# First channel product of the last batch as seven products for eight, and a newly drawn task order

## The chip, the cores and the metric

The kernel runs on one core of one Trainium2 chip. The core has five engines with an instruction queue each: TensorE (PE, matmuls, whose weight loads are shown apart as PEld), VectorE (DVE), ScalarE (ACT), GpSimd (POOL) and SyncE (SP, which here only issues transfers). Each works through its own queue in order and waits on semaphores that the others raise. The metric is the device time of one execution in microseconds, taken as the median over runs; lower is better.

## The reference

Sliding-window attention with sink tokens, then one MLP block that mixes over tokens and over channels. Batch is 4, 8 heads, 768 tokens, head size 64 (so 512 channels), 2048 hidden channels. Cut to what matters:

```python
scores = q @ k.T / sqrt(64); keep = (pos < 4) | (0 <= i - j < 128)
x   = softmax(where(keep, scores, -1e9)) @ v          # heads side by side: (4, 768, 512)
a1  = alpha1 * x + beta1
u   = x + lam * einsum('ts,bsd->btd', w_tok, a1)      # token mixing
a2  = alpha2 * u + beta2
h   = maximum(a2 @ w_ch1, 0.0)                        # first channel product, 512 -> 2048
out = u + lam * (h @ w_ch2)                           # second channel product, 2048 -> 512
```

## The kernel before

All four batches go through the same stages, and the stages of neighbouring batches overlap. Names ending in a number of batch, such as `uT3` or `hT3`, are the tiles of that batch.

- **Attention** (`scores`, `pv`): per block of 128 keys, scores go to PSUM (L724), ACT takes the exponential into `E` (L746), DVE or POOL masks it (L761, L686), PE multiplies with `vfs` (L825) and DVE divides by the sum (L850, L851) into `x`. POOL and DVE make `xh`, the input of token mixing, out of `x` (L869, L872; L860 in batch 0). In batch 0 q and k are loaded at the start, half of them by POOL's casting transfers (L497), transposed on PE (L611, L614) and copied out to `qkT` by ACT or DVE (L356, L358).
- **Token mixing** (`tok`, L956): six row tiles per batch, six matmuls of 128x512 each; DVE adds the result to `x` (L963), ACT or POOL casts it to `u16` (L356, L358). `uT` is its transpose, by PE in batch 0 (`uTp`, L997) and by transfers in the later batches; ACT or DVE then applies alpha2 and beta2 (L980, L982). A batch's 768 tokens are kept as two chunks of 384.
- **First channel product** (`mlp1`, L1036): for each chunk and each of 16 tiles of 128 hidden channels, four matmuls of 128x384 accumulate in one PSUM buffer, and one eviction on ACT (L1042) or DVE (L1044) applies the relu into `hT`. So a batch has 32 tiles and 128 matmuls. The weights are `w1f`, loaded as half precision by POOL's queue (L555).
- **Second channel product**: batch 0 does it plainly (`mlp2`, L1221). Batches 1 to 3 (`STRASSEN`) use `prod` (L1153): the product of 2x2 blocks is formed out of seven block products P1 to P7 instead of eight, with sums of blocks of `hT` (`h_sums`, S1 to S4, L1094 to L1097, all on DVE) and sums of blocks of the weights (`w2_sums`, L1068, once). P1 is read out, P2 accumulates on top of P1, and so on; DVE adds the results to `x` (L1166, L1184, L1189, L1192) and SP stores it.

The order of instructions is not written by hand. Each stage adds tasks to a `Plan` with a priority `p`, the engines that may take it with a cost for each, what it comes after, and the buffers that it uses. `Plan.run` is a list scheduler: it steps through time by those costs, and at each step takes the task that can start earliest, ties by priority, on the engine that is done with it first, giving it a free buffer. What it returns is the order in which instructions are emitted, and so the order of each engine's queue. `since`, `SEEN` and the transfer model `Rings` are part of that costing. `homes` says how many buffers there are of a kind: four PSUM banks of kind `d`, two pairs of banks of kind `S`, four buffers `n16` and four `wst`, and so on. While PE would stand idle in the first 36 us, `idle` puts in small matmuls on a tile of zeros (L349). `PAR` shifts groups of priorities, and `TURNS` is a list of seeds: `shuffle` adds random amounts to a share of the priorities, once per seed.

In the last batch nothing else is left to interleave: the program order there is token mixing among the last products of batch 2, then the 32 tiles of the first product, then the seven products of the second and the stores.

Of the kernel before, what the change touches and what calls it, by code (L numbers as in the profile page):

```python
# [9 lines left out]
FP32 = mybir.dt.float32  # L10
# [101 lines left out]
class Plan:  # L112
# [18 lines left out]

    def run(self, prio):

# [34 lines left out]
        def pick():  # L168
            best = None
            spare = {k: sorted(h for h, x in zip(homes[k], busy[k]) if not x) for k in homes}  # L170
            for r, i in open_:
                at = ready[i]
                if best is not None and at > best[0]:
                    continue
                t = tasks[i]
                asked = {}
                for b in t.uses:
                    if b.home is None:
                        asked[b.kind] = asked.get(b.kind, 0) + 1
                if any(len(spare[k]) < n for k, n in asked.items()):  # L180
                    continue
                at = max([at] + [spare[k][n - 1] for k, n in asked.items()])
                own = None
                for e in t.engs:
                    at_e = max(free[e], at)
                    if e == POOL or (e == DVE and t.port):
                        at_e = max(at_e, port)
                    key = (at_e + FW * t.engs[e], at_e, r, at_e + t.engs[e], i, e)
                    if own is None or key < own:
                        own = key  # L190
                if best is None or own[1:] < best:
                    best = own[1:]
            return best
# [51 lines left out]

    def emit(self, turns):

        prio = [t.prio for t in self.tasks]
        for seed in turns:
            prio = shuffle(prio, seed)  # L250
        for t, e, start, stop, idle in self.run(prio):
            t.at = (e, start, stop)
# [3 lines left out]
            for b in t.uses:  # L256
                if b.t is None:
                    pool, shape, dtype = self.pools[b.kind]
                    b.t = pool.tile(b.shape or shape, b.dtype or dtype,
                                    tag=f"{b.kind}_{b.home}", bufs=1, name=b.name)  # L260
            t.fn(e)


# [16 lines left out]
def kernel(  # L280
# [135 lines left out]

    TURNS = (13523, 134113, 50022, 128275, 136711, 187603, 125671, 100730, 14946, 163131, 178432, 158827, 183776, 137680, 153375, 26742, 367527, 307353, 376563, 212018, 255075, 397706, 218147, 375675, 393913, 224567, 207692, 352780, 243076, 346008)
    W1_SINCE = 20000.0
# [609 lines left out]
    def mlp1(p, b, chk, fi):  # L1028
        if fi == 0:
            hT[b, chk] = Buf("hT", None, None, f"hT{b}_{chk}")  # L1030
# [21 lines left out]
    HD = DM // 2  # L1052
    lo_, hi_ = slice(0, HD), slice(HD, DM)

    w2s = {}
# [248 lines left out]
    STEP = 100.0  # L1304
    PAR = {'lead': 50.0, 'lo0': 20, 'hi0': 16, 'lo': -20, 'hi': 30, 'lead3': 42.0, 'w2s': 10, 'p7': 2, 'hs': 0, 's2': 2, 'w2p': 9}
    for b in range(B):
# [10 lines left out]
        else:  # L1317
            seq = [("tok", ti) for ti in range(NR)]
            m1 = [("m1", 0, fi) for fi in range(NF)]
            m1 += [("m1", 1, fi) for fi in range(NF)]  # L1320
        seq += m1
        if b in STRASSEN:
            def two(u, w):
                return [("pr", a, nt) for a, nt in ((u, 0), (u, 1), (w, 0), (u, 2), (w, 1), (w, 2))]

            seq += two("P1", "P2")
            i = seq.index(("m1", 1, 8))
            seq[i:i] = [("hs", "S3")]
            i = seq.index(("pr", "P1", 0))
# [19 lines left out]
        for i, (what, *args) in enumerate(seq):  # L1349
# [6 lines left out]
            if what == "pr" and args[0] in ("P7", "P4"):  # L1356
                p -= PAR["p7"]
            {"tok": tok, "uT": uTp, "m1": mlp1, "m2": mlp2, "hs": h_sums, "pr": prod}[what](p, b, *args)
            if b and what == "tok":
                uTx(p + 0.3, b, *args)  # L1360
        if b + 1 == STRASSEN[0]:
            w2_sums(w0 + ns + PAR["w2s"])
# [30 lines left out]

    plan.emit(TURNS)

# [34 lines left out]
```

The softmax here doesn't subtract the row's maximum and nothing guards it: scores larger than these inputs give would overflow.

## Time and profile before

The median of 14 runs is 256.65 us (256.48 to 258.74). The profiled execution took 256.95 us, of which the span on the core is 255.2.

| stretch (us of the span) | what PE does there | PE busy | DVE busy | ACT busy | POOL busy |
|---|---|---|---|---|---|
| 0 to 15.46 | loads arrive, transposes, fillers | 13.24 | 10.22 | 7.79 | 7.51 |
| 15.46 to 30.49 | attention of batch 0 | 15.03 | 12.38 | 14.48 | 11.57 |
| 30.49 to 60 | token mixing and first product of batch 0 | 28.40 | 24.90 | 21.20 | 8.36 |
| 60 to 104 | rest of batch 0, attention of batch 1 | 42.83 | 34.46 | 23.34 | 17.53 |
| 104 to 212.6 | batches 1 and 2, attention and token mixing of 3 | 108.15 | 86.73 | 59.75 | 42.35 |
| 212.6 to 252 | both channel products of the last batch | 39.28 | 20.06 | 16.06 | 0.61 |
| 252 to 255.2 | last add and stores | 0.00 | 0.34 | 0.00 | 0.00 |

A line of groups gives source line, engine, operation, output and input tiles, shapes, count, then busy time and mean nanoseconds of one, and the idle time of the engine before it. The busy time of a stretch merges rows that overlap: an instruction's row can begin before the row ahead of it has ended, so durations add up to more than the time they fill. The chain of waits is the chain of work that ended last, followed back from the last instruction. In a timeline line the first figure is the start in the span, the second the length.

### The profile page before, as it was taken

What the parts mean: (1) busy time and instruction counts of PE and PEld (TensorE: products, weight loads), DVE (VectorE), ACT (ScalarE), POOL (GpSimd) and SP (SyncE); (2) the same over time, 40 slices, a digit from 0 to 9 for tenths busy, and PEclk for the clock granted to TensorE, in tenths of its full rate; (3) what the DMA queues carried; (4) which work ended last, traced back from release to release, by engine and by line L of the source; (5) the groups of instructions that cost most, each with busy time, mean ns of one, the idle gap of its engine ahead of it and who ended that gap; (6) DMA issues with size and microseconds to landing.
All of it is one profiled execution on the core that took longest, in us unless ns stands there. A gap on an engine that the chain in (4) does not pass through costs nothing.

```text
span 255.2 us, 5519 instructions
## 1 busy us (share of the span) xinstructions
PE 246.9 (97%) x2174; PEld 160.6 (63%) x2174; DVE 189.1 (74%) x402; ACT 142.6 (56%) x236; POOL 87.9 (34%) x108
## 2 busy tenths in 40 slices
PE   8899998999999999899999999999999999999994
PEld 7654645675545544456678676558668766667883
DVE  6677997596878878578889997877789764136782
ACT  2689845989848035688971225867571125775000
POOL 7409802344445330169653450735310101000000
PEclk9999999999999999999999999999999999999999
DMA  6999999998943899699679689501000256000105
GB/s 200 198 211 323 214 248 389 374 356 187 224 79 114 178 247 209 119 207 228 145 140 179 127 184 256 89 3 21 3 0 3 60 166 146 0 0 3 63 4 185
DMA packets 86130, 38.80 MB, mean 152 GB/s; under 512 B 73540, under 2 KB 80460, under 8 KB 86104
## 3 DMA queue, kind: packets, MB, share of 16 engines
q1 hardware_dynamic: 82320, 35.14, 56.5%
q0 software_dynamic: 3744, 3.28, 8.0%
q8 instruction: 17, 0.28, 0.5%
q14 instruction: 9, 0.07, 0.1%
q10 hardware_dynamic: 40, 0.03, 0.1%
HBM read 29.91 MB, written 6.29 MB: 142 GB/s over the span
## 4 chain that ended last, share of the span: by engine, by line
PE 88%; DMA 4%; DVE 3%; POOL 1%; issue 1%; ACT 1%; POOLq 0%; ACTq 0%
PE h L1036 33%; PE P L1153 21%; PE tok L956 11%; PE ch L1221 8%; PE pv L825 5%; PE S L724 4%; DMA n<-in_q_dram 4%; PE S L719 1%; DVE uT L982 1%; PE tp L614 1%; PE pv L818 1%; POOL n L497 1%; PE wT L916 1%; ACT uT L980 1%; DVE w2f L1068 1%
## 5 line engine op out<-in xcount | busy, mean ns | idle before, releaser
L1036 PE MATMUL h<-uT,w1f 128*128 128x384 f16 x512 | 91.9, 326 | 2.7 <-DVE uT L982 1.3
L1036 PEld LDWEIGHTS <-w1f 128*128 128x128 f16 x512 | 47.3, 98 | 34.4 <-issue 5.5
L1042 ACT ACTIVATE hT<-h 128x384 f16<-128x384 f32 x99 | 48.4, 493 | 25.9 <-PE h L1036 25.5
L1153 PEld LDWEIGHTS <-hT 128*128 128x128 f16 x408 | 39.8, 98 | 6.7
L746 ACT ACTIVATE E<-S 128x1024 f16<-128x1024 f32 (+1 forms) x39 | 37.9, 1001 | 7.5 <-PE S L724 3.7
L869 POOL TENSOR_TENSOR tm<-x,la_b 128x512 f32<-128x512 f32 x18 | 26.2, 1454 | 26.3 <-DVE xh L872 19.2
L956 PE MATMUL tok<-xh,wtokT 128*128 128x512 f16 x144 | 33.4, 379 | 0.0
L356 ACT CAST u<-x 128x512 f16<-128x512 f32 x19 | 11.7, 618 | 30.2 <-DVE x L963 30.0
L1153 PE MATMUL P<-w2f,hT 128*128 128x256 f16 x216 | 25.9, 273 | 0.0
L1166 DVE TENSOR_TENSOR x<-x,P 128x256 f32<-128x256 f32 x45 | 18.3, 417 | 8.2 <-PE P L1153 8.0
L1044 DVE TENSOR_SCALAR hT<-h 128x384 f16<-128x384 f32 x29 | 15.8, 553 | 11.6 <-PE h L1036 11.2
L956 PEld LDWEIGHTS <-wtokT 128*128 128x128 f16 x144 | 13.9, 98 | 14.7
L1221 PE MATMUL ch<-w2f,hT 128*128 128x512 f16 x96 | 23.0, 379 | 0.0
L1153 PE MATMUL P<-w2s,hT 128*128 128x256 f16 x192 | 22.8, 273 | 0.0
L851 DVE TENSOR_TENSOR x<-pv,rec 128x256 f32<-128x256 f32 x48 | 20.4, 424 | 1.7
L358 POOL CAST vfs<-vnat 128x512 f16<-128x512 f32 x18 | 15.0, 842 | 16.5 <-DMA vnat<-in_v_dram 16.4
L963 DVE TENSOR_TENSOR x<-x,tok 128x512 f32<-128x512 f32 x24 | 16.2, 684 | 5.7 <-PE tok L956 5.7
L356 ACT CAST n<-nat 128x768 f16<-128x768 f32 x16 | 13.2, 829 | 11.9 <-DMA nat<-in_q_dram 8.9
L825 PEld LDWEIGHTS <-E 128*128 128x128 f16 x328 | 15.2, 97 | 6.0 <-issue 1.6
L825 PE MATMUL pv<-vfs,E 128*128 128x65 f16 x328 | 17.9, 194 | 0.0
L358 POOL CAST u<-x 128x512 f16<-128x512 f32 x5 | 3.1, 622 | 34.1 <-DVE x L963 21.1
L1221 PEld LDWEIGHTS <-hT 128*128 128x128 f16 x96 | 8.6, 98 | 9.0 <-issue 0.2
(131 smaller groups left out, 325.5 us busy)
## 6 DMA issues: line engine op xcount, KB each, us to landing
out_dram<-x SPq DMA_DIRECT2D x21, 256.0 KB, 2.9
nat<-in_q_dram SPq DMA_DIRECT2D x13, 384.0 KB, 5.6
nat<-in_k_dram SPq DMA_DIRECT2D x13, 384.0 KB, 5.6
vnat<-in_v_dram SPq DMA_DIRECT2D x18, 256.0 KB, 4.8
wst_w<-in_moe_w_ch_dram SPq DMA_DIRECT2D x8, 512.0 KB, 7.8
wtn<-in_moe_w_tok_dram SPq DMA_DIRECT2D x6, 384.0 KB, 4.2
w1f<-in_moe_w_ch_dram POOLq DMA_DIRECT2D x4, 512.0 KB, 10.1
v<-in_v_dram SPq DMA_DIRECT2D x12, 128.0 KB, 7.0
```

The costliest lines, as they stand in the source:

```text
L356: nc.scalar.copy(o, i)
L358: engine[e].tensor_copy(o, i)
L746: nc.scalar.activation(eT.t, pS.t[:, :, 0 : n * w].rearrange("p e (i w) -> p e i w", i=n), AF.Exp, scale=scale)
L825: nc.tensor.matmul(po.t[:, hl, :], eT.t[:, e_, off + i, c : c + P], vf[j][:, h, :], start=(r < 2 and n == 0), stop=(n == len(parts) - 1 an ...
L851: nc.vector.tensor_mul(bx.t[:, 4 * G : 4 * G + 4, :], po.t[:, :, 0:D], rec.t.to_broadcast([P, 4, D]))
L869: engine[e].tensor_mul(bt.t, bx.t.rearrange("p h d -> p (h d)"), la1_b)
L956: nc.tensor.matmul(pt.t, wtokT[:, si, ti * P : (ti + 1) * P], hs[si].t, start=(si == 0), stop=(si == NR - 1))
L1036: nc.tensor.matmul(ph.t, w1f[:, c, fi * P : (fi + 1) * P], bu.t[:, c, chk * NTOK : (chk + 1) * NTOK], start=(c == 0), stop=(c == NC - 1))
L1042: nc.scalar.activation(bh.t[:, fi, :], ph.t, AF.Relu)
L1153: nc.tensor.matmul(pc.t, hh[:, nt * P : (nt + 1) * P], w(fi), start=(first and n_ == 0), stop=(n_ == HF - 1), skip_group_check=True)
L1166: nc.vector.tensor_add(row(bx)[:, cols], row(bx)[:, cols], pc.t)
L1221: nc.tensor.matmul(pc.t, bh.t[:, fi, nt * P : (nt + 1) * P], w2f[:, fi, :], start=(fi == 0), stop=(fi == NF - 1))
```

## The change

In the last batch (`HSUM = 3`) the first channel product is done as seven products for eight too, for six of the eight pairs of hidden tiles. A pair is tile i and tile i + 8 for both chunks, so a 2x2 block product: two hidden tiles, two chunks, the 512 channels in two halves. The tiles 0, 1, 8 and 9 (`NPL = 2`) stay as they were, through `mlp1`.

- `w1_sums` makes S1 to S4 of blocks of `w1f`, eight instructions of 128x768. S1, S2 and S4 go to three buffers of kind `wst`; S3 is written into `w1f` in place, so it comes after the last tile of batch 2 that reads the same columns.
- `u_sums` makes T1 to T4 of blocks of `uT`, four instructions of 128x768, into the four `n16` buffers.
- `mlp1_pair` adds the seven products of a pair, each of two matmuls of 128x384. P1, P6, P5 and P3 accumulate one after another in one PSUM bank (V); P1, P6 and P5 are read out into buffers `ha`, `hb` and `hc` (kinds `vnat` and `x`) before the next may accumulate. P7 and P4 share the other bank of the pair (Q), P2 has a buffer of kind `d`. DVE adds `ha` to P2, `hc` to P7 and `hb` to P7 + P4 into `hT`, each followed by a relu in place on DVE, POOL or ACT; P3's bank is evicted with a relu as before.
- In the last batch S3 of the second product is placed before P1 instead of among the tiles.
- The order: `Plan.run` takes a list `pin` that can bind a task to one of its engines, a new function `nudge` changes priorities and pins from a seed, and the kernel lists 188 such seeds (`NUDGES`). `TURNS` differs from the seventeenth seed on, and `PAR` has other values. All tasks of the kernel are reordered by this, those of the start included: POOL's first casting load of q comes ahead of its work on `sel`, SP's first load is q instead of a tile of w_tok, ACT takes seven of the eight copies to `qkT` of batch 0 (five before) and three of six to `wtokT` (two before). Of the eight sums of `w1f`, six stand among the token adds of batch 1 and two among those of batch 3.

The engine totals of the program: 500 matmuls of 128x384 for the first product (512 before), 99 fillers (106), 429 instructions on DVE (399), 240 on ACT (242), 130 on POOL (113). The source lines move: L1036 becomes L1088, L1153 becomes L1326; the 84 matmuls of the pairs are L1181.

```diff
--- before.py
+++ after.py
@@ -129,7 +129,7 @@
-    def run(self, prio):
+    def run(self, prio, pin=None):
         tasks = self.tasks
         rank = [0] * len(tasks)
@@ -181,7 +181,10 @@
                     continue
                 at = max([at] + [spare[k][n - 1] for k, n in asked.items()])
                 own = None
-                for e in t.engs:
+                one = pin[i] if pin and pin[i] <= len(t.engs) else 0
+                for n, e in enumerate(t.engs):
+                    if one and n + 1 != one:
+                        continue
                     at_e = max(free[e], at)
                     if e == POOL or (e == DVE and t.port):
                         at_e = max(at_e, port)
@@ -243,12 +246,15 @@
         self.ends = free
         return steps
-    def emit(self, turns):
+    def emit(self, turns, nudges):
         prio = [t.prio for t in self.tasks]
         for seed in turns:
             prio = shuffle(prio, seed)
-        for t, e, start, stop, idle in self.run(prio):
+        pin = [0] * len(prio)
+        for seed in nudges:
+            nudge(prio, pin, seed)
+        for t, e, start, stop, idle in self.run(prio, pin):
             t.at = (e, start, stop)
...
+def nudge(prio, pin, seed):
...
+    kind = mix() % 6
+    w = wide[mix() % 8]
+    c = mix() % n
+    def by():
+        a = unit()
+        return (a + unit() - 1.0) * w
+    if kind == 0:
+        prio[c] += by()
+    elif kind == 1:
+        for _ in range(2 + mix() % 5):
+            i = (c + mix() % 60) % n
+            prio[i] += by()
...
+    elif kind == 4:
+        pin[c] = mix() % 3
+    else:
+        prio[c] += by()
+        i = (c + mix() % 30) % n
+        pin[i] = mix() % 3
 def shuffle(prio, seed):
@@ -414,7 +465,8 @@
     PAIRS = 3
-    TURNS = (13523, 134113, 50022,
...
-        26742, 367527, 307353, 376563,
...
-        243076, 346008)
+    TURNS = (13523, 134113, 50022,
...
+        26742, 354967, 310655, 266923,
...
+        392681, 339225)
+    NUDGES = (514892687, 622207306, 64711582,
...
+        192761335, 155598846)
     W1_SINCE = 20000.0
     V0 = (((0, 1), (2, 3), (4, 5)), ((0, 1, 2), (3, 4, 5)))
@@ -1026,7 +1078,7 @@
                 [done["uTd", b, 3 * chk + i] for i in range(3)] + [done["ab2"]], [bo])
     def mlp1(p, b, chk, fi):
-        if fi == 0:
+        if (b, chk) not in hT:
             hT[b, chk] = Buf("hT", None, None, f"hT{b}_{chk}")
         bh, bu = hT[b, chk], uT[b, 0]
         ph = Buf("d", [P, NTOK], FP32, f"h{b}_{chk}_{fi}")
@@ -1051,6 +1103,127 @@
     HF = NF // 2
     HD = DM // 2
     lo_, hi_ = slice(0, HD), slice(HD, DM)
+    HSUM = 3
+    NPL = 2
+    w1s = {}
+    uS = {}
+    pair = {}
+    def w1_sums(p):
+        n = (HF - NPL) * P
+        f, k_ = slice(NPL * P, HF * P), slice((HF + NPL) * P, NF * P)
+        for w in ("S1", "S2", "S4"):
+            w1s[w] = Buf("wst", [P, 2, n], FP16, f"w1{w}")
+        b1, b2, b4 = w1s["S1"], w1s["S2"], w1s["S4"]
+        late = [done["h", HSUM - 1, chk, fi] for chk in range(2) for fi in range(HF + NPL, NF)]
+        for c in range(2):
+            def sub(q, name, made, after, uses, c=c):
+                done["w1" + name, c] = add(
+                    p + 4 * c + q, {DVE: 600, POOL: 2000}, lambda e: made(engine[e], c), after, uses, port=True)
+            sub(0, "S1", lambda g, c: g.tensor_add(b1.t[:, c], w1f[:, c, k_], w1f[:, 2 + c, k_]), [done["w1", 3]], [b1])
+            sub(1, "S2", lambda g, c: g.tensor_sub(b2.t[:, c], b1.t[:, c], w1f[:, c, f]), [done["w1S1", c]], [b1, b2])
+            sub(2, "S4", lambda g, c: g.tensor_sub(b4.t[:, c], w1f[:, 2 + c, f], b2.t[:, c]), [done["w1S2", c]], [b2, b4])
+            sub(3, "S3", lambda g, c: g.tensor_sub(w1f[:, c, k_], w1f[:, c, f], w1f[:, c, k_]),
+                [done["w1S1", c]] + late, [])
+    def u_sums(p, b):
+        bu = uT[b, 0]
+        for w in ("T1", "T2", "T3", "T4"):
+            uS[w] = Buf("n16", [P, 2, NTOK], FP16, f"u{w}")
+        t1, t2, t3, t4 = (uS[w] for w in ("T1", "T2", "T3", "T4"))
+        c0, c1 = slice(0, NTOK), slice(NTOK, S)
+        ud = lambda chk, h: [done["uT", b, chk, 2 * h + c] for c in range(2)]
+        def sub(q, name, made, after, uses):
+            done["u" + name] = add(p + q, {DVE: 500, POOL: 1500}, lambda e: made(engine[e]), after, [bu] + uses, port=True)
+        sub(0, "T3", lambda g: g.tensor_sub(t3.t, bu.t[:, 2:4, c1], bu.t[:, 0:2, c1]), ud(0, 0) + ud(1, 0) + ud(1, 1), [t3])
+        sub(0.1, "T1", lambda g: g.tensor_sub(t1.t, bu.t[:, 0:2, c1], bu.t[:, 0:2, c0]), ud(0, 0) + ud(1, 0), [t1])
+        sub(0.2, "T2", lambda g: g.tensor_sub(t2.t, bu.t[:, 2:4, c1], t1.t), [done["uT1"]] + ud(1, 1), [t1, t2])
+        sub(0.3, "T4", lambda g: g.tensor_sub(t4.t, bu.t[:, 2:4, c0], t2.t), [done["uT2"]] + ud(0, 1), [t2, t4])
+    def mlp1_pair(p, b, what, i):
+        if what == "P1":
+            for chk in range(2):
+                if (b, chk) not in hT:
+                    hT[b, chk] = Buf("hT", None, None, f"hT{b}_{chk}")
+            pair[i] = [Buf("S", None, None, f"hp{i}"), Buf("d", [P, NTOK], FP32, f"h{b}_0_{i}")] + [
+                Buf(k_, [P, NTOK], FP32, f"h{w}{i}") for k_, w in (("vnat", "a"), ("vnat", "b"), ("x", "c"))]
+        two, px, ba, bb, bc = pair[i]
+        bu = uT[b, 0]
+        f, k_ = slice(i * P, (i + 1) * P), slice((HF + i) * P, (HF + i + 1) * P)
+        fs = slice((i - NPL) * P, (i - NPL + 1) * P)
+        c0, c1 = slice(0, NTOK), slice(NTOK, S)
+        lhs, rhs, after, into, uses = {
+            "P1": (lambda c: w1f[:, c, f], lambda c: bu.t[:, c, c0], [done["w1", i // 4]], "V", []),
+            "P2": (lambda c: w1f[:, 2 + c, f], lambda c: bu.t[:, 2 + c, c0], [done["w1", i // 4]], "X", []),
+            "P3": (lambda c: w1s["S4"].t[:, c, fs], lambda c: bu.t[:, 2 + c, c1], [done["w1S4", c] for c in range(2)], "V", [w1s["S4"]]),
+            "P4": (lambda c: w1f[:, 2 + c, k_], lambda c: uS["T4"].t[:, c], [done["uT4"]], "Q", [uS["T4"]]),
+            "P5": (lambda c: w1s["S1"].t[:, c, fs], lambda c: uS["T1"].t[:, c], [done["uT1"]] + [done["w1S1", c] for c in range(2)], "V", [w1s["S1"], uS["T1"]]),
+            "P6": (lambda c: w1s["S2"].t[:, c, fs], lambda c: uS["T2"].t[:, c], [done["uT2"]] + [done["w1S2", c] for c in range(2)], "V", [w1s["S2"], uS["T2"]]),
+            "P7": (lambda c: w1f[:, c, k_], lambda c: uS["T3"].t[:, c], [done["uT3"]] + [done["w1S3", c] for c in range(2)], "Q", [uS["T3"]]),
+        }[what]
+        if what in ("P1", "P2", "P3"):
+            after = after + [done["uT", b, what == "P3", c] for c in ((0, 1) if what == "P1" else (2, 3))]
+        first = what in ("P1", "P2", "P7")
+        po = px if into == "X" else two
+        def acc():
+            return px.t if into == "X" else two.t[:, "VQ".index(into), 0:NTOK]
+        def mm(e):
+            for c in range(2):
+                nc.tensor.matmul(acc(), lhs(c), rhs(c), start=first and c == 0, stop=c == 1, skip_group_check=True)
+        before = {"P6": "P1", "P5": "P6", "P3": "P5", "P4": "P7"}.get(what)
+        if before:
+            after = after + [done["hread", before, i]]
+        if what == "P7":
+            after = after + [done["hp", "P1", i]]
+        a = done["hp", what, i] = add(p, {PE: 2 * 163}, mm, after, [po, bu] + uses)
+        def read(bx):
+            return add(p + 0.05, {ACT: 493, DVE: 556}, lambda e: copy(e, bx.t, acc()), [a], [po, bx])
+        def plus(bx, chk, fi, more, acc=acc):
+            bh = hT[b, chk]
+            r = add(p + 0.05, {DVE: 556}, lambda e: nc.vector.tensor_add(bh.t[:, fi, :], bx.t, acc()), [a] + more, [po, bx, bh])
+            def relu(e):
+                if e == ACT:
+                    nc.scalar.activation(bh.t[:, fi, :], bh.t[:, fi, :], AF.Relu)
+                else:
+                    engine[e].tensor_scalar_max(bh.t[:, fi, :], bh.t[:, fi, :], 0.0)
+            done["h", b, chk, fi] = add(p + 0.06, {DVE: 300, POOL: 600, ACT: 493}, relu, [r], [bh], port=True)
+            return r
+        if what == "P1":
+            done["hread", "P1", i] = read(ba)
+        elif what == "P2":
+            plus(ba, 0, i, [done["hread", "P1", i]])
+        elif what == "P6":
+            done["hread", "P6", i] = read(bb)
+        elif what == "P5":
+            done["hread", "P5", i] = r = read(bc)
+            done["hread", "P7", i] = plus(bc, 1, HF + i, [r, done["hp", "P7", i]], lambda: two.t[:, 1, 0:NTOK])
+        elif what == "P4":
+            plus(bb, 0, HF + i, [done["hread", "P6", i]])
+        elif what == "P3":
+            bh = hT[b, 1]
+            def relu(e):
+                if e == ACT:
+                    nc.scalar.activation(bh.t[:, i, :], acc(), AF.Relu)
+                else:
+                    nc.vector.tensor_scalar_max(bh.t[:, i, :], acc(), 0.0)
+            done["h", b, 1, i] = add(p + 0.05, {ACT: 493, DVE: 556}, relu, [a], [po, bh])
     w2s = {}
@@ -1302,7 +1475,7 @@
     STEP = 100.0
-    PAR = {'lead': 50.0, 'lo0': 20, 'hi0': 16, 'lo': -20, 'hi': 30, 'lead3': 42.0, 'w2s': 10, 'p7': 2, 'hs': 0, 's2': 2, 'w2p': 9}
+    PAR = {'lead': 46.0, 'lo0': 20, 'hi0': 16, 'lo': -12, 'hi': 26, 'lead3': 58.0, 'w2s': -20, 'p7': 2, 'hs': 3, 's2': 0, 'w2p': 9, 'mp': 1.3, 'us': 15, 'w1s': -30}
     for b in range(B):
         w0 = STEP * b
         if b == 0:
@@ -1318,14 +1491,23 @@
             seq = [("tok", ti) for ti in range(NR)]
             m1 = [("m1", 0, fi) for fi in range(NF)]
             m1 += [("m1", 1, fi) for fi in range(NF)]
+            if b >= HSUM:
+                own = [fi for h in range(2) for fi in range(HF * h, HF * h + NPL)]
+                m1 = [("m1", chk, fi) for chk in range(2) for fi in own] + [("us",)]
+                order = ("P1", "P7", "P2", "P6", "P5", "P4", "P3")
+                m1 += [("mp", w, i) for i in range(NPL, HF) for w in order]
         seq += m1
         if b in STRASSEN:
             def two(u, w):
                 return [("pr", a, nt) for a, nt in ((u, 0), (u, 1), (w, 0), (u, 2), (w, 1), (w, 2))]
+            i = len(seq)
             seq += two("P1", "P2")
-            i = seq.index(("m1", 1, 8))
-            seq[i:i] = [("hs", "S3")]
+            if b < HSUM:
+                i = seq.index(("m1", 1, 8))
+                seq[i:i] = [("hs", "S3")]
+            else:
+                seq[i:i] = [("hs", "S3")]
             i = seq.index(("pr", "P1", 0))
             seq[i:i] = [("hs", "S1")]
             seq += two("P7", "P4")
@@ -1355,9 +1537,17 @@
                 p -= PAR["hs"] if args[0] == "S3" else PAR["s2"]
             if what == "pr" and args[0] in ("P7", "P4"):
                 p -= PAR["p7"]
-            {"tok": tok, "uT": uTp, "m1": mlp1, "m2": mlp2, "hs": h_sums, "pr": prod}[what](p, b, *args)
+            if b >= HSUM and len(args) == 2 and what == "mp":
+                p = start + 3.6 * (args[1] - NPL) + PAR["mp"] * order.index(args[0])
+            elif b >= HSUM and what == "us":
+                start = p
+                u_sums(p - PAR["us"], b)
+                continue
+            {"mp": mlp1_pair, "tok": tok, "uT": uTp, "m1": mlp1, "m2": mlp2, "hs": h_sums, "pr": prod}[what](p, b, *args)
             if b and what == "tok":
                 uTx(p + 0.3, b, *args)
+        if b + 1 == HSUM:
+            w1_sums(w0 + ns + PAR["w1s"])
         if b + 1 == STRASSEN[0]:
             w2_sums(w0 + ns + PAR["w2s"])
         if b + 1 < B:
@@ -1391,7 +1581,7 @@
                 else:
                     pv(p, nb, *args)
-    plan.emit(TURNS)
+    plan.emit(TURNS, NUDGES)
 # ---- launch: one core; inputs and outputs as the reference has them ----
```

## The prediction

> **What bounds the kernel now.** I read the share of each engine first, then the stages as windows, then the chain of waits, then VectorE's (DVE's) instructions in order of time. In the windows the columns are the stretch, its length, and the busy time of PE, PEld, DVE, ACT and POOL with instruction counts, then the granted clock.
>
> ```profile
> PE 246.9 (97%) x2174; PEld 160.6 (63%) x2174; DVE 189.1 (74%) x402; ACT 142.6 (56%) x236; POOL 87.9 (34%) x108
> ```
>
> ```profile
> 15.46:30.49 15.03, 15.03 (x214) 8.73 (x215) 12.38 (x37) 14.48 (x24) 11.57 (x16) 1.00 1.03 259
> ...
> 97.00:104.00 7.00, 5.83 (x28) 2.54 (x26) 5.82 (x12) 3.41 (x6) 0.64 (x1) 1.00 0.92 192
> ...
> 104.00:212.60 108.60, 108.15 (x959) 73.82 (x957) 86.73 (x179) 59.75 (x98) 42.35 (x43) 1.00 0.54 114
> 212.60:252.00 39.40, 39.28 (x297) 28.85 (x295) 20.06 (x39) 16.06 (x33) 0.61 (x1) 1.00 0.16 48
> ```
>
> ```profile
> 212.74 20.80 PE h L1036 x128
> 233.54 18.35 PE P L1153 x168
> 251.92 0.42 DVE x L1166
> ```
>
> ```profile
> 189.83 0.96 DVE L1095 TENSOR_TENSOR hT<-hT 128x1536 f16<-128x1536 f16 x1 [0.20 <-ACT hT L1042]
> ...
> 195.10 0.95 DVE L1097 TENSOR_TENSOR hT<-hT 128x1536 f16<-128x1536 f16 x1
> 195.96 0.41 DVE L1166 TENSOR_TENSOR x<-x,P 128x256 f32<-128x256 f32 x1
> ...
> 217.47 1.25 DVE L982 TENSOR_SCALAR uT<-uT,ab 128x384 f16<-128x384 f16 x4 [4.00 <-DMA uT<-u]
> ```
>
> From 104 us on, PE is the bound: 0.45 us idle in 108.6, and none in the first product of the last batch (128 matmuls in 20.80 us, 0.1625 each), nor to speak of in the second (168 in 18.35, 0.109 each). What PE no longer does there is worth its full time, as long as the others keep up; and in the last 39.4 us DVE is half idle (20.06) and POOL wholly. Before 31 us the bound is mixed: ACT is busy 14.48 of 15.03 us, POOL and DVE little less. PE has two real holes later, 1.11 us at 38.7 to 42 and 1.17 us at 97 to 104, both where a batch passes from token mixing to its first product.
>
> **The change part by part.**
>
> *Removed on PE.* Six tile pairs take 14 matmuls for 16: 12 of 128x384, 12 x 0.1625 = **-1.95 us**. The built order holds it: 116 such matmuls in the last batch. Seven fillers of the start go too; they fill waits and count for nothing.
>
> *Added on DVE, ACT and POOL.* Each pair had four evictions of about 0.49 (ACT, L1042) or 0.55 (DVE). It gets three reads (17 of 18 on ACT, 0.49), three adds of a read and a PSUM bank (DVE; between 0.417 at 256 columns and 0.684 at 512, so 0.55), three in-place relus (8 on POOL, 6 on DVE, 4 on ACT) and one relu out of PSUM. An in-place relu on DVE is bounded by 0.227 (256 columns, constants) and 0.38 (384, the row of four above); I take 0.31. On POOL, by 0.39 (affine_select of 256) and 0.67 (of 512); I take 0.55. Four sums of uT go to DVE, 0.56 each (between 0.435 at 512 columns and 0.95 at 1536).
>
> Does DVE keep up? In the built order 62 DVE instructions stand between the start of pair 5's first matmul and the last S2 sum that the second product's P6 waits for: 18 adds (9.9 us), 8 sums of hT (7.9), 4 of uT (2.3), 6 relus (1.9), 4 PSUM evictions (2.2), 2 affines (1.0), 20 adds of second products (8.9), in all 34.1. PE's share of the same stretch is 116 x 0.1625 + 136 x 0.109 = 33.7. But rows overlap: the sum at 195.10 lasts 0.95 and the next starts after 0.86; the four affines take 1.25 where one takes 0.38. At 0.08 less each, DVE needs 34.1 - 62 x 0.08 = 29.1, or 86% of PE's time. From 189.8 to 200 DVE runs with hardly a gap beside a PE that never stops, so 86% can be carried.
>
> The remaining question is order. Stepping through the last batch with full row lengths, waiting at each read, PE reaches pair 6 after 21.0 us for 20.7 of work, the P6 of the second product after another 13.3 for 13.0 (pairs 6 and 7 wait 0.1 to 0.2 for the reads between their chained products, since only each other cover them; then about 0.1 for S2), and the end after 9.6 for 9.6: **+0.6 us**. Bounds: 0, if the overlap takes it up; 3.6, if each of six pairs bares one read and its hand-off (0.49 + 0.1). I take 0.6, nearest to the walk. The tail stays, one add (0.42) and the same stores.
>
> A pair's chain queues more than itself: PE is in order, so a product that waits for its read holds the plain tiles and the P1 of the second product behind it; on DVE an add that waits for hc holds the S3 and S1 sums, which P7 waits for.
>
> *Eight sums of w1.* Six now stand among the token adds at the hole of 97 to 104, two at the end of batch 2. Between the add of the last token tile that chunk 0 needs and its last affine, DVE has about 6.9 us of rows (3 sums of w1 at 0.56 among them), PE 5.6 to 6.1 us of work: a stall near 0.9 in place of 1.17. At 38.7 the four transposes now run ahead of the first h and fill 0.66 more of the hole, but the last waits for token tile 3's add and cast (0.68 + 0.62): about 0.9 for 1.11. Together **-0.4 us**, bounds -1.0 and +1.7 (all three w1 sums bare). The other two sums lie in DVE's gaps between the second products of batch 2 (0.2 to 0.9 us each in 200 to 212).
>
> *The start, reordered.* POOL's first casting load of q, which waited for the memset of sel until 1.83 and issued at 2.47, now goes first, and SP's first load is q, not a 384 KB tile of w_tok (1.9 us at the 200 GB/s of this stage). PE's first transposes could come 1.9 us earlier. Against it: from 15.46 on ACT is full, and two more qkT evictions and one of wtokT (0.80 each) are put on it; POOL takes an lb1 product (1.27) ahead of the last q load. I take **-0.5 us**, bounds -1.9 and +1.0.
>
> *The rest.* All priorities are drawn anew. In 104 to 212.6 there is 0.45 us to win, and more to lose: **+0.2**, bounds -0.45 and +1.5. SP's queue keeps its 136 issues.
>
> Sum: -1.95 + 0.6 - 0.4 - 0.5 + 0.2 = -2.05. The profiled execution took 256.95 (span 255.2 and 1.75 around it), 0.3 above the median of 256.65; so 254.9 against that execution, **254.6** for the median.
>
> *Two rules against the row.* The S3 sum at 186.58 took 1.58 for 0.95 while POOL ran a product from 186.08 to 187.35, so a POOL operation cost DVE 0.63 once; eight such hits would be 5.0 us, and DVE's 29.1 would pass PE's 33.7 by 0.4. The Trainium skill (SBUF — State Buffer, "Who interferes with whom") says a DVE instruction with two SBUF inputs and a GpSimd one that reads SBUF shut each other out for a whole instruction. By that rule alone each POOL relu could hold one sum for its full length, an estimate of 4 to 5 us on DVE; it speaks against the relus on POOL.
>
> Short waits between groups of two matmuls might also cost clock. The granted clock is 1.00 in 97 to 104 in spite of 1.17 us of idle PE. The same skill (TensorE: Matmul & The Clock Gate, "A second HAM failure mode: psum-queue depth-cycling") says small idles between matmul groups can make the clock fall to half and back; one of its windows of 3.4 us at half speed would be an estimate of 1.7 us lost. The row decides: nothing.
>
> **Rivals.**
>
> *The pairs' chain becomes the bound (slower).* P1, read, P6, read, P5, read, P3 and relu are in series, and two PSUM pairs let only two chains run. If every pair bares one read and hand-off, 6 x 0.6 = 3.6 us, and nothing else is won: 256.65 - 1.95 + 3.6 = **258.3**. It decides from 0.33 us per pair, 1.95 / 6. For it: ACT's row is one every 0.65 us today, PE never waits on a chain. Against: a chain needs 4 x 0.325 + 3 x 0.59 + 0.5 = 3.6 us, two at a time 1.8 per pair, and PE has 2.3 per pair and 5.2 us of plain tiles between. Chance 0.18.
>
> *The saving is eaten (no change).* Stalls of 1.0 in the pairs and a start that ACT holds where it is, with 0.7 of new holes elsewhere: -1.95 + 1.7 = -0.25, **256.4**. For it: ACT's 14.48 of 15.03. Chance 0.14.
>
> *The start brings all (faster).* 1.9 from the loads, 0.8 from the two holes, 0.3 lost in pairs: -1.95 + 0.3 - 0.8 - 1.9 = -4.35, **252.3**. For it: PE waits 0.88 for q's first casting load. Against: ACT. Chance 0.13.
>
> **How the numbers follow.** My forecast has 0.55; its own range is 253.2 to 256.0. A measurement tells about 0.2% (0.5 us) from no change. Faster: nearly all of mine, 0.13, and 0.06 of the eaten case, 0.72; slower: 0.17 of the chain, 0.03 else, 0.20; same 0.08. The range 252.5 to 258.0 leaves out half of the fast rival and less than half of the slow one.
>
> **What would show it.** Right: the stretch from the last token tile to the end shortens by 1.2 to 1.9 us, h and hp matmuls together about 18.9 us of the chain, no wait of PE on ACT or DVE over 0.3 in the pairs, first transposes of q before 7 us, the first token matmul before 30.4. Wrong: reads ending PE's waits pair after pair; S sums well over 0.95 beside POOL's relus; a hole above 1.2 us at the start of batch 1; token mixing of batch 0 later than 30.4.

## The result, and the profile after

The changed kernel takes 257.98 us (median), the kernel before 256.71 in the same comparison: a ratio of 1.0055, with a 95% interval of 1.0042 to 1.0068. It is slower by about 1.3 us where 2.0 less was forecast. The profiled execution took 258.81 us, 0.83 above the median; its span is 256.9 us, against 255.2 before.

The engine totals of the changed kernel:

```profile
PE 245.8 (96%) x2155; PEld 158.8 (62%) x2155; DVE 207.2 (81%) x432; ACT 143.0 (56%) x238; POOL 106.5 (41%) x125
```

The same stretches as windows (stretch, its length, then the busy time of PE, PEld, DVE, ACT and POOL). The first boundary is the one used before; the second, 32.06, is the first matmul of token mixing (30.37 before). The last two stretches are the last batch, from the first matmul of a pair to PE's last, divided where the pairs end:

```profile
0.00:15.46 15.46, 12.89 (x179) 9.67 (x181) 9.48 (x33) 8.15 (x13) 10.35 (x24) 1.00 1.02 201
15.46:32.06 16.60, 15.47 (x214) 8.81 (x210) 12.43 (x37) 15.99 (x24) 11.38 (x16) 1.00 1.04 260
...
97.00:104.00 7.00, 6.43 (x31) 2.87 (x30) 6.16 (x13) 3.19 (x7) 2.56 (x3) 1.00 0.89 147
104.00:206.71 102.71, 102.43 (x904) 68.54 (x903) 85.56 (x173) 59.30 (x98) 42.56 (x45) 1.00 0.56 111
206.71:235.90 29.19, 27.05 (x183) 17.56 (x181) 22.51 (x49) 15.43 (x33) 11.18 (x9) 1.00 0.16 56
235.90:253.54 17.64, 17.62 (x161) 15.56 (x159) 15.73 (x32) 1.36 (x4) 0.00 (x0) 1.00 0.21 73
```

PE is idle for 2.1 us among the pairs, where it had no idle time before, and for none after them. Busy time of a pipelined PE hides short stalls, so I also counted work. From the first pair's matmul to PE's last, 46.82 us pass. The 340 matmuls in them are 43.27 us of work (0.1625 per matmul of 384 columns and 0.109 per matmul of 256, the prediction's rates). So **3.55 us are stall**; the prediction had 0.6. The kernel before has no such stall; PE is busy for 45.22 of the last 45.34 us up to 252:

```profile
206.66:252.00 45.34, 45.22 (x335) 32.46 (x332) 24.52 (x49) 17.97 (x37) 1.25 (x2) 1.00 0.22 65
```

The same count over the head, with all matmuls but the fillers, each at the rate of its shape in the chain's rows: the changed kernel is behind by 1.7 us at 32, by 1.1 at 60, by 0.3 at 104 and by 0.3 at 206. So it starts token mixing late, wins most of that back in the two holes at 38 to 43 and 97 to 104, and enters the last batch nearly even. The loss of the whole is made in the pairs.

The 1.7 at 32 us is partly this one execution. In the four other profiles below whose start has the same order, token mixing begins at 30.77 to 31.39; in the five with the start of before (the kernel before among them, and leaving out the execution of 503 us told below) at 29.99 to 30.45.

Where in the pairs, the chain of waits shows (start, length, what ran; the part from the last plain tile to the second product, without pieces under 0.04 us):

```profile
226.96 0.34 PE hp L1181 x2
227.34 0.04 issue
227.39 0.10 DVE hT L1195
227.49 0.37 issue
227.86 0.56 DVE hT L1224
228.42 0.04 issue
228.46 0.82 PE hp L1181 x4
229.31 0.49 ACT ha L407
229.80 0.04 issue
229.84 0.82 PE hp L1181 x4
230.70 0.04 issue
230.74 0.49 ACT ha L407
...
234.04 0.38 ACT pt L407
234.44 0.57 DVE hT L1195
235.03 0.50 ACT hT L1222
235.53 0.04 issue
235.57 0.48 PE hp L1181 x2
236.06 17.48 PE P L1326 x160
```

And the waits of PE in 206 to 237 us, with total, count and longest:

```profile
PE hp L1181 <- ACT ha L407: 0.8, 3, 0.3
PE hp L1181 <- ACT hT L1222: 0.6, 1, 0.6
PE hp L1181 <- DVE hT L1224: 0.5, 1, 0.5
PE hp L1181 <- ACT hb L407: 0.2, 1, 0.2
```

Two of these should not exist by the code. L1222 and L1224 are the relu of P3, which empties bank V, and nothing that follows it on PE in its own pair needs it: the matmuls that wait are P4, which accumulates in bank Q. The three waits for `ha` are no better: the product that waits in each of them is P7, which opens bank Q, while `ha` is read from bank V. The built program says the same. Its waits for pair 7, access by access:

```
P7   (PE, writes Q)    waits for the read of ha    (ACT, reads V)
add  (DVE, hc + Q)     waits for P3                (PE, writes V)
relu (ACT, of P3 in V) waits for the add of hc     (DVE, reads Q)
P4   (PE, adds to Q)   waits for the relu of P3    (ACT, reads V)
```

V and Q are two PSUM banks, but one buffer of kind `S`. The framework that places the semaphores orders all accesses to this buffer by different engines, reads against reads too, as they stand in the program. What was meant as two chains side by side is one: P5, hc, P3, add, relu, P4, add.

### The profile page after: what moved, and what is told of

Same layout as the page of the kernel before. It is cut to its first block, busy times and chain, and to the rows that moved or that the text cites. A ratio compares the mean times of both kernels' runs of the same rounds, so it can differ in the third digit from the quotient of the medians.

```text
span 256.9 us, 5541 instructions
## 1 busy us (share of the span) xinstructions
PE 245.8 (96%) x2155; PEld 158.8 (62%) x2155; DVE 207.2 (81%) x432; ACT 143.0 (56%) x238; POOL 106.5 (41%) x125
## 4 chain that ended last, share of the span: by engine, by line
PE 55%; DVE 3%; ACT 1%; issue 1%; DVEq 0%; ACTq 0%
PE P L1326 22%; PE h L1088 17%; PE tok L1008 6%; PE hp L1181 4%; PE pv L877 2%; PE S L776 2%; DVE E L813 1%; PE h L1181 1%; ACT ha L407 1%; PE pv L763 0%; DVE x L903 0%; DVE x L1015 0%; DVE hT L1195 0%; PE sk L708 0%; DVE hT L1224 0%
## 5 line engine op out<-in xcount | busy, mean ns | idle before, releaser
L1088 PE MATMUL h<-uT,w1f 128*128 128x384 f16 x416 | 75.7, 326 | 0.6 <-DVE uT L1034 0.6
L1088 PEld LDWEIGHTS <-w1f 128*128 128x128 f16 x416 | 38.5, 98 | 25.2 <-issue 2.8
L1094 ACT ACTIVATE hT<-h 128x384 f16<-128x384 f32 x77 | 37.4, 494 | 27.8 <-PE h L1088 27.4
L1326 PEld LDWEIGHTS <-hT 128*128 128x128 f16 x408 | 39.6, 98 | 6.7 <-issue 0.4
L1326 PE MATMUL P<-w2f,hT 128*128 128x256 f16 x216 | 25.7, 273 | 0.0
L1326 PE MATMUL P<-w2s,hT 128*128 128x256 f16 x192 | 22.9, 273 | 0.0
L1096 DVE TENSOR_SCALAR hT<-h 128x384 f16<-128x384 f32 x27 | 14.9, 554 | 7.4 <-PE h L1088 6.9
L409 POOL CAST vfs<-vnat 128x512 f16<-128x512 f32 x18 | 12.8, 727 | 15.3 <-DMA vnat<-in_v_dram 15.3
L738 POOL TENSOR_SCALAR_AFFINE_SELECT E<-E 128x512 f16<-128x512 f16 x16 | 10.6, 685 | 15.2 <-ACT E L798 15.2
L1201 POOL TENSOR_SCALAR hT<-hT 128x384 f16<-128x384 f16 x8 | 9.9, 1244 | 15.2 <-PE hp L1181 8.3
```

Of the source, the lines that this page charges most:

```text
L1088: nc.tensor.matmul(ph.t, w1f[:, c, fi * P : (fi + 1) * P], bu.t[:, c, chk * NTOK : (chk + 1) * NTOK], start=(c == 0), stop=(c == NC - 1))
L1094: nc.scalar.activation(bh.t[:, fi, :], ph.t, AF.Relu)
L1326: nc.tensor.matmul(pc.t, hh[:, nt * P : (nt + 1) * P], w(fi), start=(first and n_ == 0), stop=(n_ == HF - 1), skip_group_check=True)
```

## The experiments

The order of the changed kernel is kept in most of these. Where single steps were moved, the order that the planner had drawn was written out as a list (number of the task, letter of its engine, its new buffers; `i` for fillers) and emitted from it, so that nothing else is drawn anew:

```diff
-        for t, e, start, stop, idle in self.run(prio, pin):
+        for t, e, idle in self.listed():
```

| kernel | us | of before, same comparison | ratio | 95% interval |
|---|---|---|---|---|
| after the change | 257.98 | 256.71 | 1.0055 | 1.0042 to 1.0068 |
| banks apart | 255.23 | 256.64 | 0.9956 | 0.9940 to 0.9971 |
| POOL's relus on VectorE | 258.20 | 256.64 | 1.0071 | 1.0057 to 1.0085 |
| head of after, plain last batch | 256.75 | 256.64 | 1.0003 | 0.9987 to 1.0019 |
| start of before | 256.72 | 256.64 | 1.0013 | 0.9999 to 1.0026 |
| last q load first | 258.52 | 256.65 | 1.0075 | 1.0048 to 1.0102 |
| two copies on VectorE | 257.58 | 256.67 | 1.0030 | 1.0016 to 1.0044 |
| w_tok tile first | 258.20 | 256.67 | 1.0068 | 1.0042 to 1.0095 |
| banks apart, start of before | 253.99 | 256.65 | 0.9885 | 0.9859 to 0.9912 |
| the same, once more | 253.85 | 256.57 | 0.9888 | 0.9872 to 0.9905 |
| the same, POOL's relus on VectorE | 254.09 | 256.57 | 0.9900 | 0.9885 to 0.9915 |
| banks apart, POOL's relus on VectorE | 254.83 | 256.69 | 0.9927 | 0.9915 to 0.9939 |
| banks apart, order searched again | 256.78 | 256.69 | 1.0006 | 0.9997 to 1.0016 |

Theories at the start: the shared buffer; against it the chain of reads by its mere length (the prediction's first rival), POOL's relus, and the new order of the head.

### Banks apart

After the last scores the pool of kind `S` is closed, and one with four single banks is opened in its place. Instructions and their order on every engine stay.

```diff
+    def banks(b):
+        if not two_banks:
+            psS_ctx.close()
+            two_banks.append(ctx.enter_context(tc.tile_pool(name="psV", bufs=1, space=bass.MemoryType.PSUM)))
+        return [two_banks[0].tile([P, 512], FP32, tag=f"{k_}_{b.home}", bufs=1, name=f"{b.name}_{k_}") for k_ in "VQ"]
...
-            return px.t if into == "X" else two.t[:, "VQ".index(into), 0:NTOK]
+            return px.t if into == "X" else two.t["VQ".index(into)][:, 0:NTOK]
```

> The same order of instructions, engine by engine; only the two PSUM banks of a pair (V for P1, P6, P5, P3, and Q for P7, P4) become two buffers instead of one of kind S, in a pool opened after the last scores. If the shared buffer is the cause (its accesses wait for one another in the order of the program: P7 for the read of P1, the add of hc for P3, the relu of P3 for that add, P4 for that relu), 2 to 3 of the 3.4 us that PE loses in the last batch come back: 255.0 to 256.0. If the chain of reads by itself or POOL's slow relus are the cause, no change: 257.8 to 258.2.

255.23 us, 2.75 less than the changed kernel and 0.44% faster than before. Of PE's waits in 206 to 237 us, one is left:

```profile
PE hp_V L1194 <- ACT hb L420: 0.2, 1, 0.2
```

The windows of the same two stretches of it:

```profile
206.15:233.00 26.85, 26.66 (x187) 18.02 (x185) 23.31 (x51) 15.23 (x34) 11.20 (x9) 1.00 0.17 61
233.00:250.20 17.20, 17.15 (x158) 15.13 (x155) 15.22 (x32) 1.34 (x3) 0.00 (x0) 1.00 0.22 75
```

From the first pair to PE's last matmul 44.00 us pass for the same 43.27 of work: 0.74 of stall in place of 3.55. In the built program P4 of pair 7 now waits for the add of hc, the relu of P3 for P3, the add for the read of hc, and P7 for the last add of pair 2, which had the bank before. The shared buffer is the cause, shown by taking it alone away. The reads between the chained products are all still there, in the same places, and P1, P6, P5 and P3 of a pair still wait for each other; so their mere length was not the cause.

### POOL's relus on VectorE

```diff
-                    engine[e].tensor_scalar_max(bh.t[:, fi, :], bh.t[:, fi, :], 0.0)
+                    nc.vector.tensor_scalar_max(bh.t[:, fi, :], bh.t[:, fi, :], 0.0)
```

> The same order, but the eight in-place relus that stand on POOL (1.24 us each) are issued on VectorE at the same places (0.26 each). If POOL's relus are the cause, by holding the hidden tiles back or VectorE out of SBUF, 2 to 3 us come back: 255.0 to 256.0. If the shared PSUM buffer or the chain of reads is the cause, within 0.5 of 258.0, rather 0.2 less than more.

258.20: no gain. The relus are far dearer on POOL than I took them (the changed kernel's groups, count, busy time, mean ns and idle time before):

```profile
L1201 POOL TENSOR_SCALAR hT<-hT 128x384 f16<-128x384 f16 x8 | 9.9, 1244 | 15.2 <-PE hp L1181 8.3 <-DVE hT L1195 6.8
```

```profile
L1201 DVE TENSOR_SCALAR hT<-hT 128x384 f16<-128x384 f16 x6 | 1.6, 264 | 0.2
```

Yet nobody is late for it. The same exchange was made twice more, on top of the banks apart, and of the banks and the start together (both told below):

> The changed kernel's order with the banks apart, and the eight relus of POOL issued on VectorE at the same places. With the shared buffer gone, POOL's relus (1.24 us for the 0.55 that the prediction took) could show: if they hold the sums of hT back, 0.3 to 0.8 less than 255.23. If VectorE, busy 87% in the pairs, is nearer to being the bound, 0.2 to 0.8 more. If neither, within 0.2.

> All that has paid so far: the two banks of a pair as buffers of their own, the start in the order of the kernel before, and the eight relus of POOL on VectorE. If the relus' gain on the banks alone (254.83 against 255.23, in different comparisons) is real and adds up, 253.4 to 253.8; if it was the scatter between comparisons, 253.9 to 254.2.

254.83 against 255.23 in two comparisons on two chips, with intervals that just miss each other (up to 0.9939 and from 0.9940), but 254.09 against 253.85 side by side on one chip. So POOL's relus cost nothing that can be measured, with the shared buffer or without it.

### The head of the changed kernel with a plain last batch

```diff
+    PAIRED = False
...
-            if b >= HSUM:
+            if b >= HSUM and PAIRED:
```

> The order of the changed kernel up to the first instruction of a pair; from there the last batch is done plainly, 32 tiles of four matmuls, in the order of the kernel before. Six of the eight sums of w1 stay where they are; the two in-place ones (S3) are left out, since the plain tiles need those columns. If the loss lies in the pairs, the head costs what the traces say, 0.2 us: 256.6 to 257.1. If the new order of the head were the cause, 258 or more.

256.75 with a ratio of 1.0003: as expected if the loss lies in the pairs. The head, with six of the eight sums of `w1f` in it, costs nothing that can be measured.

### The start of before

The first 157 steps (up to the first matmul of token mixing) from the kernel before, the others in the changed kernel's order.

```diff
-6s0 7s1 8g2 10s0 5g 11s 9g3 16s 17s 0g 12g4 45d0 13g5
+27s0 6s0 5g 7s1 8g2 10s0 9g3 11s 16s 0g 12g4 75d0 17s
...
```

> The changed kernel with the order of the kernel before up to the first matmul of token mixing (157 steps), and its own order from there. If the start is worth what the two traces say (token mixing begins 1.7 us later after the change, of which part is covered by the hole that follows), 0.7 to 1.5 us come back: 256.5 to 257.3. If the start's delay is covered by later waits, within 0.3 of 258.0.

256.72, 1.26 us less than the changed kernel. So the new start costs 1.1 us (by the ratios) to 1.3 (by the medians), and the rest of the new head wins about as much. Three runs looked for the step that does it.

> The changed kernel with one step moved: POOL issues the last casting load of q (head pair 3) ahead of the masks, as the kernel before does, and not behind the product of lb, where it stands after the change and is issued at 10.81 instead of 6.03 (it lands at 17.6 instead of 15.4). If this one step in POOL's queue is the start's delay, 0.8 to 1.4 us come back, as with the whole start put back (256.72): 256.6 to 257.2. If the delay is in the copies given to ACT or in the other loads, within 0.4 of 258.0.

```diff
-47a0 18s 1g 48d1
+47a0 18s 14g6 1g 48d1
```

258.52: no gain. The load is issued at 6.08 instead of 10.81 and lands at 14.29 instead of 17.60, but its transposes keep their place in PE's queue, and what follows is as late as before. My chain of reasons for this run stopped at the load.

> The changed kernel with two of the seven copies to qkT that stand on ACT at the start (the k tile of head pair 2 and the q tile of head pair 3 of batch 0, 0.80 us each) issued on VectorE at the same places; nothing else moves. If ACT's full queue from 7 to 31 us is the start's delay, these 1.6 us of ACT come back in good part: 256.5 to 257.3. If the delay is in the loads or in the token weights' tile that is no longer cast early, within 0.4 of 258.0.

```diff
-58a
+58d
...
-60a
+60d
```

257.58: 0.4 us by the medians, 0.6 by the ratios. The intervals of the two ratios just overlap (up to 1.0044 here, from 1.0042 with the whole new start), so ACT's copies are likely a part, but it is not shown.

> The changed kernel with four steps moved to where the kernel before has them: SP loads one tile of w_tok first of all, and its cast, its transposes and its copy (0.94 and 0.56 on VectorE or ACT) are done before 7 us, while the engines wait for loads, and not between 28 and 33. The first loads of q and k come 0.45 us later for it. If the delay of token mixing is the work that stands last ahead of it, 0.5 to 1.4 us come back: 256.6 to 257.5. If it is ACT's copies or the loads, within 0.4 of 258.0, or slower by the later q.

```diff
-6s0 7s1 8g2 10s0 5g 11s 9g3 16s 17s 0g 12g4 45d0 13g5 46p0i1,37 47a0
+27s0 6s0 7s1 8g2 10s0 5g 11s 9g3 16s 17s 0g 12g4 75d0 45d1 13g5 76p0i1,35 77d 46p2 47a0
```

258.20: no gain, though token mixing begins at 30.90 in the profile of this run (an execution of 257.48). That lies within the scatter of the unchanged start, 30.77 to 32.06. Half of the start's cost or more stays open; it may take several of these steps together, which was not tried.

### Both undone

> The two banks of a pair as buffers of their own, and the start in the order of the kernel before. If the two causes are independent and add up, 255.23 - 1.26 = 254.0: 253.6 to 254.4. If the pairs' stalls had hidden part of the start's delay, or the other way round, 254.6 to 255.2.

253.99, and the two causes add up: 255.23 - 1.26 = 253.97. One of the six executions took 503.43 us; without it the median is 253.87. The profile is of that execution. In it a matmul of 384 columns takes 556 ns for 326, and PE is busy for 496.7 us, where VectorE has its usual 208.1; the granted clock reads 1.00. No run here shows why.

The same kernel once more, for its profile and beside the one with POOL's relus on VectorE:

> The same kernel as in the run with the banks apart and the start of before, once more beside the one with the relus on VectorE, for a comparison on one chip and a profile of it: 253.7 to 254.3 if the first measurement holds.

253.85, ratio 0.9888 (0.9872 to 0.9905): 1.1% faster than the kernel before, and the best of the study. Its waits of PE from 30 us to the end:

```profile
PE uTp L1070 <- DVE uT L1055: 1.0, 1, 1.0
PE h L1109 <- DVE uT L1055: 0.6, 1, 0.6
PE pv L898 <- DVE E L834: 0.3, 1, 0.3
PE hp_V L1202 <- ACT hb L430: 0.2, 1, 0.2
```

What is left of waits is at the holes of 38 and 97 us (1.0 and 0.6), 0.3 before a `pv` of the attention, and 0.2 in the pairs.

### The order searched again

All steps after the start were moved about at random, keeping what the planner's model called shorter, with POOL's relu at 1.2 us in that model and the banks apart.

> The two banks of a pair as buffers of their own, the start in the order of the kernel before, and the rest of the order searched again with the same planner, told 1.2 us for a relu on POOL and that it doesn't hold VectorE back. The planner promises 1.5 us over the order of the changed kernel with that start. If its costs hold, 252.3 to 253.2; if they hold in part only, as with the order of the changed kernel, 253.2 to 254.0; if the new order runs into waits that the planner doesn't know, above 254.0.

256.78: 2.8 us worse than the order it began from, where the planner had promised 1.5 better. Its chain of waits near the end:

```profile
244.94 1.07 issue
246.01 1.27 POOL x L1386
247.28 0.02 issue
247.31 0.43 DVE x L1360
247.74 0.04 issue
247.78 3.67 PE P L1347 x32
```

The search had put an add of the second product on POOL, where the planner has 0.76 us for it; the chip takes 1.27, after 1.07 for which the profile shows no cause. A chain of waits does not say that PE stands still meanwhile, and it does not: it is busy all the time, and waits 0.2 us at the end. The window, and PE's largest waits from 30 us on:

```profile
242.50:247.70 5.20, 5.20 (x48) 4.53 (x47) 4.08 (x8) 0.00 (x0) 3.60 (x3) 1.00 0.14 47
...
PE uTp L1070 <- ACT u L430: 1.5, 1, 1.5
PE hp_V L1202 <- DVE uT L1055: 0.8, 1, 0.8
PE tp L687 <- ACT n L430: 0.6, 1, 0.6
...
PE P L1347 <- DVE x L1360: 0.2, 1, 0.2
```

PE's waits add up to 3.9 us, against 2.1 in the order that the search began from, and from PE's last matmul to the end 4.2 us pass, against 3.4. That is 2.6 of the 3.4 us between the two profiled spans (255.6 and 252.2). The add on POOL shows one cost that the model has too low; that this made the loss is not shown, and the loss is spread over several places.

## Why the prediction was wrong

**The step that failed is the "+0.6 us" for the order of the last batch.** It came from stepping through the built order with the dependences that the code states: V and Q as two banks that are filled and read independently. With the banks apart that walk holds, 0.74 us for 0.6. In the program as built they are one buffer, and the stall is 3.55, just inside the upper bound of 3.6. That bound had been reckoned for another mechanism (each pair bares one read), so it was right by its size alone, which is luck.

*The first rival* gave 258.3 with the chain as the bound, and the time came out at 257.98. Its mark, "reads ending PE's waits pair after pair", is seen: three waits for `ha`. But its reason against itself, that two chains run side by side, was right by the code and only failed by the shared buffer. The wait to look for was not one for a late read. It was one for an access that has no data to give, and the waits in the built order name it before any run: P4 waiting for ACT's or DVE's relu of P3.

*Removed on PE, -1.95*: right. The last batch has 116 matmuls of 384 columns, and with the stall gone the kernel is faster than before.

*VectorE's load*: right. I had 86% of PE's time from the first pair to the last S2; with the banks apart it is busy for 23.31 of 26.85 us over the pairs, 87%, and PE waits once, for ACT.

*The in-place relus*: 0.264 on VectorE for 0.31 taken. On POOL 1.24 (most are 1.16, one 1.81), for 0.55 taken and a bound of 0.67. The bound was from `affine_select` rows, the nearest ones, and they are not the same operation. It had no effect on the time.

*The rule on VectorE and POOL*: by the Trainium skill (SBUF — State Buffer, "Who interferes with whom") the prediction had an estimate of 4 to 5 us lost on VectorE to POOL's relus. None of it came: the eight sums of hT in the last batch took 0.95 each. But only two of the eight stood beside a relu of POOL. The relu that POOL began at 229.62, 0.16 us after VectorE had begun a sum, took 1.81 for 1.16, so there POOL gave way. The sum that VectorE began at 232.02, while the next relu ran (231.40 to 232.56), kept its time, and so did that relu. A product on POOL that began first did hold VectorE, as before the change: a sum of batch 2 took 1.77, and an affine of uT took 1.21 for 0.37 at 208.64, while POOL ran a product of 128x512 (208.47 to 209.73).

```profile
L1267 DVE TENSOR_TENSOR hS<-hT,hT 128x1536 f16<-128x1536 f16 x2 | 1.9, 952 | 0.0
...
187.82 1.26 POOL L921 TENSOR_TENSOR tm<-x,la_b 128x512 f32<-128x512 f32 x1 [1.58 <-DVE xh L924]
188.12 1.77 DVE L1267 TENSOR_TENSOR hS<-hT,hT 128x1536 f16<-128x1536 f16 x1 [0.39 <-ACT hT L1094]
```

Taking all relus off POOL won nothing.

*The rule on the clock* didn't apply either: the granted clock is 1.00 through the pairs, with 2.1 us of short idle times in them. By itself that settles little, since it also reads 1.00 in the execution of 503 us; but the pairs' matmuls of 384 columns take 325 to 326 ns, as before the change (326).

*The holes, -0.4*: better than forecast. PE's idle time in them fell from 1.11 and 1.17 us to 1.00 and 0.57, 0.7 together, inside the bounds. By the count of work the changed kernel makes up 0.6 us at 38 to 43 and 0.8 at 97 to 104, 1.4 in all and past the bound of -1.0; the rest may be only the late start, which leaves less to wait for.

*The start, -0.5*: wrong in sign. The first transposes of q did come before 7 us (4.72), but token mixing starts at 32.06 in the profile, not before 30.4. I had named the reason against it, "two more qkT evictions" on a full ACT, and set it too low: the whole start costs 1.1 to 1.3. Two of ACT's copies put back gave 0.4 to 0.6 of that, at the edge of what the intervals can tell; the rest stays open.

*The rest, +0.2*: about 0 by the count of work between 104 and 206 us.

Sum against the profile: -1.95 + 3.55 + 1.7 (start) - 1.4 (holes) + 0 = +1.9, for 1.7 of span. What the count leaves over, 0.2, may lie in the rates that it uses. The 1.7 is this execution's; by the medians the change is +1.3.

## What to carry to other kernels

Before a change that lets two engines work on two banks at once is costed, read in the built program what each access waits for: two banks in one buffer may be ordered as one, and the remedy, two buffers, moves no instruction and was worth 2.75 us here. An order found by searching a planner's model need not bring what the model promises (1.5 us better promised, 2.8 worse measured); hold each stage's measured time against the time that the planner gave it, and look first where the two part. A step moved earlier in one queue won nothing here while the next step kept its place in another. A chain of waits names what released what, not what stood idle: look at the engine's own busy time before calling it a stall.

## What was unexpected of the hardware

An in-place relu of 128x384 half-precision values took POOL 1.16 us as a rule and VectorE 0.26, a factor of 4.4. POOL's `affine_select` on 128x512 takes 0.69 in the same run, so the time of one operation on POOL says little about another's.

Between VectorE's sums of two SBUF tiles and POOL it mattered who began first. Beside a sum that was already running, a product on POOL took 1.91 for 1.27 (at 129.40) and a relu 1.81 for 1.16 (at 229.62); beside a product on POOL that was already running, a sum took 1.77 for 0.95 (at 188.12). A relu on POOL that had begun 0.6 us earlier held no sum.

The order among the accesses to one PSUM buffer that the program keeps is stricter than what the chip was seen to need. The Trainium skill (PSUM — Partial Sum Buffer, "PSUM bank collisions raise a hardware error") says that two engines may not be at the same bank at once, reads against reads included, so an order by bank has a reason; by its rule two banks need none. The run with the banks apart agrees: ACT, VectorE and PE worked on V and Q without an order between the two, and 2.75 us came back.
